# Retention steps of a fused retention and MoE kernel, placed by a written table instead of by run-ahead counters

## The chip, the core and the metric

The kernel runs on one core of a Trainium2 chip. A core has engines that each run their own instructions in order and wait for each other by semaphores: TensorE (PE in the profile; its weight loads are PEld), VectorE (DVE), ScalarE (ACT), GpSimd (POOL) and SyncE (SP). Transfers between device memory and on-chip memory (SBUF) are issued by SP, and here also by ACT, and run on 16 shared DMA engines. TensorE writes its results to the accumulation memory (PSUM), from which VectorE and ScalarE read them.

The metric is the device time of one execution in microseconds (us). The kernel before took 311.57 us, the median of 11 runs (310.76 to 315.99).

## The reference: what is computed

```python
scores = scale * np.matmul(q, k.transpose(0, 1, 3, 2))     # 8 batches, 8 heads, 576 positions, 64 wide
Dmat = np.where(rel >= 0, gamma[:, None, None] ** rel[None, :, :], 0.0)
attn = np.matmul(scores * Dmat[None], v)                   # retention: causal, decaying with distance
x = attn.transpose(0, 2, 1, 3).reshape(B * S, H * D)       # 4608 tokens, 512 wide
h = x @ w_in                                               # 512 -> 2048
g = h * np.clip(h + 3.0, 0.0, 6.0) / 6.0                   # hard swish
out = g @ w_out                                            # 2048 -> 512
```

Inputs and outputs are float32; inside, matrix operands are float16.

## The kernel before

**Retention by chunks.** Each of 8 batches has 576 positions: four chunks of 128 and a tail of 64. Two batches' tails make one tail chunk, so there are 36 chunks in `order` (0 to 35; 14, 23, 32 and 35 are tails). The decay is split into a factor on q and one on k and v, so that a chunk needs a causal mask and, from its second chunk of a batch on, a carried state. The steps of one chunk i have a letter each in what follows:

- **l**: three loads of q, k, v into tile `st` (SP, line 93; six of 64 rows for a tail, line 98). Six `st` buffers.
- **c**: three casts with the decay factors into `qk16` and `v16` (POOL, line 113). Five buffers of each.
- **x**: one DMA transpose of `qk16` into `qkT`, issued by ACT (line 121). Four buffers. The first eight chunks go through TensorE instead.
- **s** (`ret1`): 8 small matmuls to `sc` (line 150), then the mask on VectorE into `at` (line 157). `sc` has one buffer, so the next s waits for this mask.
- **o** (`ret2`): the matmuls of `at` with v and of the state with q into `xp` (lines 172, 178, 185), the state's update (line 197), then copies of `xp` into `xt` (line 202) and of the state (line 208) on ACT, or on VectorE for a batch's last chunk (line 210).

**The MoE by blocks.** 512 tokens make a block: block b holds the four full chunks of batch b, block 8 all tails. Blocks run in the order 0 to 6, 8, 7. Block 0 is done plainly, under the start-up loads. Each other block has an up part of 16 units and seven products:

- An up unit is 8 (`up_half`, 256 columns each, blocks 1 and 2) or 4 (`up`, 512 columns, the others) matmuls into one `mm` buffer of PSUM (lines 255, 241), then on ACT `u` (line 224) and on VectorE `g` (line 229). There are four `mm` buffers, shared with the products.
- The products P1, P5, P6, P2, P7, P4, P3 (line 353) are a Strassen form of the down matrix product: 16 matmuls each. Some need sums of g, made by `enc(kb, which, j0, j1)` on VectorE (line 317): written **e**kb.which.j0.j1 below. P5 reads sum 1, P6 sum 2 (which needs sum 1), P7 sum 3, P3 sum 4 (which needs sum 2). P5, P6, P7, P4 also read `tmat` 0 to 3, differences of the weights that `tbuild` makes once on VectorE (line 444): **t**2 and **t**3 fall into block 1. After P1 ACT copies X (line 359); after P6, P7, P4, P3 VectorE adds W, Z and the outputs (lines 362, 368, 376, 379, 382); after P2 ACT copies an output (line 373). Each of the last four products issues a store from SP (line 386).

**What sets the order.** The kernel is recorded under a manual schedule: each engine gets its instructions in the order in which the program writes them. Before, that order comes from counters: `burst()` writes s of chunk i+1, o of chunk i and then `ahead()`, which writes transposes up to three chunks ahead and casts up to four ahead, each cast followed by a load (`do_cast`, `do_load`). `burst` is called at fixed places: after up units 5 and 11, after some products (the sets given to `down`), and by `catch_up`. The sums of g stand at fixed places too. Each DMA of SP and ACT also takes one of eight completion counters in turn and waits until the earlier DMA on that counter has landed.

Of the kernel before, what the change touches and what calls it, by code (L numbers as in the profile page):

```python
# [18 lines left out]


E_H0, E_H = 316, 256
E_TAIL = 544


@with_exitstack
def kernel(
# [18 lines left out]
    NFC = DFF // P  # L45
# [96 lines left out]
    def ret1(c, nwarm=0):  # L142
        kind, b, t = c
        qt = qkTs[c]
        sc = psum.tile([P, 2, HP, P], FP32, tag="sc", name="sc")
        if nwarm:
            warm(sc[:, 0, 0, :], nwarm)
        for p in range(HP):
            for z in range(2):
                nc.tensor.matmul(sc[:, z, p, :],  # L150
                                 qt[z * D:z * D + D, HP + p, :],
                                 qt[z * D:z * D + D, p, :],
                                 start=True, stop=True)
# [3 lines left out]
        nc.vector.tensor_tensor(  # L157
            out=at.rearrange("p z a i -> p (z a) i"),
            in0=sc.rearrange("p z a i -> p (z a) i"),
            in1=m[:, :].unsqueeze(1).to_broadcast([P, 2 * HP, P]),  # L160
            op=ALU.mult)
# [134 lines left out]
    HF = NFC // 2  # L296
# [136 lines left out]
    def tbuild(which):  # L433
        if which == 0:
            a, c = wq(0, 1), wq(0, 0)
        elif which == 1:
            a, c = wq(1, 1), tmat[0]
        elif which == 2:
            a, c = wq(1, 1), wq(0, 1)
        else:  # L440
            a, c = wq(1, 0), tmat[1]
        for h in range(2):
            s = slice(4 * h, 4 * h + 4)
            nc.vector.tensor_tensor(out=tmat[which][:, s, :], in0=a[:, s, :],
                                    in1=c[:, s, :], op=ALU.subtract)


    order = []
# [6 lines left out]
    NCHK = len(order)  # L455
# [17 lines left out]
    for h in range(H):  # L473
        e = eq0 if h == 0 else eq
# [30 lines left out]
    def do_cast():  # L505
        if ncast[0] < NCHK:
            for ix in range(3):
                cast(order[ncast[0]], ix, GP)
            ncast[0] += 1
            do_load(ncast[0] + 6)  # L510

    def do_xp(tag=None, eng="v"):
        if nxp[0] < NCHK:
            if tag:
                xpose_pe(order[nxp[0]], tag, eng)
            else:
                xpose(order[nxp[0]])
            nxp[0] += 1

    def r1(i, nwarm=0):  # L520
        if i < NCHK:
            while nxp[0] <= i:
                do_xp()
            ret1(order[i], nwarm)

    def r2():
        if nb[0] < NCHK:
            ret2(order[nb[0]])
            nb[0] += 1

    def ahead():

        i = nb[0] - 1
        while nxp[0] < NCHK and nxp[0] <= i + 3 and nxp[0] < ncast[0]:
            do_xp()
        while ncast[0] < NCHK and ncast[0] <= i + 4:
            do_cast()

    def burst():
        if nb[0] < NCHK:  # L540
            r1(nb[0] + 1)
            r2()
            ahead()

    def catch_up(n):
        while nb[0] <= n:
            burst()


    c0 = order[:4]  # L550
# [66 lines left out]
            r2()  # L617
    down_plain_end(0, pos)
    do_xp("xp", "s")
    ahead()  # L620
    for w in range(8):
        up_half(1, 0, (w, w + HF))
        if w == 1:
            r1(7)
            r2()
            ahead()
        if w == 5:
            r2()
            ahead()
    for w in range(8):  # L630
        up_half(1, 1, (w, w + HF))
        if w == 1:
            ahead()
        if w in (4, 7):
            enc(1, 1, 0 if w == 4 else 4, 4 if w == 4 else 8)

    def down(kb, slots):
        enc(kb, 2, 0, 8)
        if kb >= 3:
            enc(kb, 3, 4, 8)  # L640
        for nm in ("P1", "P5", "P6", "P2", "P7", "P4", "P3"):
            product(kb, nm)
            if nm in slots:
                burst()
            if nm == "P1" and kb < 3:
                enc(kb, 3, 0, 8)
            if nm == ("P5" if kb > 1 else "P2"):
                enc(kb, 4, 0, 8)
            if kb == 1:
                if nm == "P1":  # L650
                    tbuild(2)
                if nm == "P5":
                    r1(8)
                if nm == "P6":
                    tbuild(3)

    def up_block(kb, slots):
        catch_up(need[kb])
        for fx in range(NFC):
            up(kb, (fx // 2) + (fx % 2) * HF)  # L660
            if fx in slots:
                burst()
            if fx == 9:
                enc(kb, 3, 0, 4)
                enc(kb, 1, 0, 4)
        enc(kb, 1, 4, 8)

    down(1, ("P7", "P4"))
    for w in range(8):
        up_half(2, 0, (w, w + HF))  # L670
        if w in (1, 5):
            burst()
    catch_up(need[2])
    for w in range(8):
        up_half(2, 1, (w, w + HF))
        if w in (4, 7):
            enc(2, 1, 0 if w == 4 else 4, 4 if w == 4 else 8)
    down(2, ("P1", "P6", "P2", "P7", "P4"))
    for kb in (3, 4, 5, 6, 8, 7):
        up_block(kb, (5, 11) if kb < 7 else ())  # L680
        down(kb, {3: ("P1", "P2"), 4: ("P1", "P2", "P4"), 5: ("P1", "P2"),
                  6: ("P1", "P6", "P2", "P7", "P4")}.get(kb, ()))


# [1 line left out]
_INS = ['q', 'k', 'v', 'moe_w_in', 'moe_w_out']  # L686
_OUTS = [((4608, 512), 'float32')]
# [25 lines left out]
```

## Time and profile before

| what | value |
|---|---|
| median of 11 runs | 311.57 us |
| the profiled execution: its own time | 313.4 us |
| its span, first to last instruction | 311.7 us |
| PE busy | 289.7 us (93%) |
| DVE busy | 234.3 us (75%) |
| ACT busy | 147.3 us (47%) |
| POOL busy | 119.6 us (38%) |
| mean granted TensorE clock | 0.989 |

The profile of one execution gives each engine's busy time, the waits (who waited for whom, by the semaphore that came last), the chain of work that ended last, a timeline of each engine, and tables by window. A matmul's busy time includes its pipeline, so single durations (273 ns for a 256-column matmul) are longer than the rate at which they follow each other (16 of them in 1.75 us). The stages of the profiled execution, read off PE's timeline: block 0 until 58.1 us, block 1 from 58.1 to 92.25, block 2 to 131.1, block 3 to 161.4, block 4 to 192.8, block 5 to 223.35, block 6 to 255.4, block 8 to 281.5, block 7 to 307.65, then the last output and its store.

### The profile page before, as it was taken

The page shows a single profiled execution, that of the slowest core. Times are in us where ns is not written, and L with a number is a line of the kernel's source. Part 1 is how long each engine was busy: PE and PEld are TensorE (multiplying, and loading weights), DVE is VectorE, ACT ScalarE, POOL GpSimd, SP SyncE. Part 2 cuts the span into 40 slices and gives each one's busy share as a digit, 9 for nine tenths or more (in the row PEclk, how much of TensorE's full clock was granted, in tenths as well). Part 3 has the DMA queues.
Part 4 walks back from the last instruction along what each step waited for, and adds up shares of the span by engine and source line. Part 5 has one row for each costly group of instructions (what it writes and reads, how often), then busy time and mean ns, then how long its engine had stood idle before and what let it go on. Part 6 is the DMA issues. An engine that isn't in the chain of part 4 may idle for free.

```text
span 311.7 us, 7065 instructions
## 1 busy us (share of the span) xinstructions
PE 289.7 (93%) x2848; PEld 199.5 (64%) x2848; DVE 234.3 (75%) x311; ACT 147.3 (47%) x277; POOL 119.6 (38%) x131
## 2 busy tenths in 40 slices
PE   1679999979999998799999999999999999999994
PEld 0465445768788886545874587458746874685583
DVE  4745749649978997489968986799689857956963
ACT  5474664746136733176327632763176326505610
POOL 5217518957175577533446327334610000000000
PEclk9988999999999999799999999999999999999999
DMA  9999999999999999999999999992511120014003
GB/s 167 218 350 387 377 207 216 203 186 225 255 203 199 230 216 207 249 188 188 206 212 206 220 243 175 242 210 47 170 34 36 36 105 33 1 27 102 8 2 135
DMA packets 155937, 53.94 MB, mean 173 GB/s; under 512 B 143104, under 2 KB 151296, under 8 KB 155904
## 3 DMA queue, kind: packets, MB, share of 16 engines
q1 hardware_dynamic: 126336, 46.15, 70.5%
q10 hardware_dynamic: 29568, 7.34, 18.2%
q8 instruction: 22, 0.36, 0.5%
q14 instruction: 11, 0.09, 0.1%
HBM read 36.70 MB, written 9.44 MB: 148 GB/s over the span
## 4 chain that ended last, share of the span: by engine, by line
PE 64%; DMA 12%; DVE 10%; issue 4%; SPq 4%; ACT 3%; POOL 1%; ACTq 0%; POOLq 0%
PE ph L241 24%; PE accC L353 9%; PE accB L353 7%; PE accA L353 7%; PE ph L255 5%; DMA st<-in_k_dram 5%; SPq L93 4%; PE accD L353 3%; DMA wst<-in_moe_w_out_dram 3%; DVE ss L317 3%; PE xp L172 3%; PE sc L150 3%; DMA qkT<-qk 2%; DVE at L157 2%; DMA st<-in_v_dram 2%
## 5 line engine op out<-in xcount | busy, mean ns | idle before, releaser
L229 DVE SCALAR_TENSOR_TENSOR g<-u,ph 128x512 f16<-128x512 f32 x144 | 95.6, 685 | 29.5 <-ACT u L224 28.7
L224 ACT ACTIVATE u<-ph 128x512 f32<-128x512 f32 x144 | 84.1, 597 | 67.8 <-PE ph L241 52.2
L241 PE MATMUL ph<-xt,win 128*128 128x512 f16 x384 | 85.6, 380 | 0.1
L241 PEld LDWEIGHTS <-win 128*128 128x128 f16 x448 | 43.3, 98 | 50.2 <-issue 0.6
L113 POOL TENSOR_TENSOR qk<-st,tq 128x512 f16<-128x512 f32 x30 | 32.9, 1096 | 61.2 <-issue 32.0
L113 POOL TENSOR_TENSOR v<-st,tkv 128x512 f16<-128x512 f32 x36 | 40.3, 1120 | 39.0 <-DMA st<-in_v_dram 22.3
L353 PEld LDWEIGHTS <-ss 128*128 128x128 f16 x512 | 49.5, 99 | 8.1 <-DVE ss L317 0.8
L157 DVE TENSOR_TENSOR at<-sc,mask 128x1024 f16<-128x1024 f32 x32 | 39.0, 1218 | 6.5 <-PE sc L150 6.2
L353 PEld LDWEIGHTS <-g 128*128 128x128 f16 x384 | 37.2, 98 | 5.7
L113 POOL TENSOR_TENSOR qk<-st,tkv 128x512 f16<-128x512 f32 x30 | 34.5, 1150 | 1.8 <-DMA st<-in_k_dram 1.8
L202 ACT ACTIVATE xt<-xp 128x512 f16<-128x512 f32 x32 | 19.2, 598 | 29.5 <-PE xp L178 25.3
L353 PE MATMUL accB<-tmat,ss 128*128 128x256 f16 x256 | 30.6, 273 | 0.7 <-DVE W L362 0.4
L255 PE MATMUL ph<-xt,win 128*128 128x256 f16 x256 | 29.1, 273 | 1.9 <-DVE g L229 1.9
L353 PE MATMUL accA<-wout,g 128*128 128x256 f16 x256 | 30.6, 273 | 0.0
L255 PEld LDWEIGHTS <-win 128*128 128x128 f16 x256 | 24.7, 98 | 5.0 <-issue 2.1
L317 DVE TENSOR_TENSOR ss<-g 128x1024 f16<-128x1024 f16 (+1 forms) x30 | 24.8, 843 | 0.3
L172 PE MATMUL xp<-at,v 128*64 128x128 f16 x288 | 20.7, 232 | 2.5 <-DVE at L157 2.5
L150 PE MATMUL sc<-qkT 64*128 64x128 f16 x288 | 14.9, 226 | 5.0 <-DMA qkT<-qk 2.1
L172 PEld LDWEIGHTS <-v 128*64 128x64 f16 x288 | 14.7, 114 | 6.8 <-issue 2.8
L373 ACT COPY osb<-accA 128x512 f32<-128x512 f32 x8 | 4.7, 586 | 29.6 <-PE accA L353 29.6
L150 PEld LDWEIGHTS <-qkT 64*128 64x128 f16 x288 | 8.6, 97 | 14.8 <-issue 9.7
L208 ACT CAST s<-state 64x256 f16<-64x256 f32 x48 | 17.3, 360 | 0.5
(61 smaller groups left out, 271.7 us busy)
## 6 DMA issues: line engine op xcount, KB each, us to landing
st<-in_q_dram SPq DMA_DIRECT2D x32, 256.0 KB, 5.3
st<-in_k_dram SPq DMA_DIRECT2D x32, 256.0 KB, 5.9
st<-in_v_dram SPq DMA_DIRECT2D x32, 256.0 KB, 6.4
out_dram<-osb SPq DMA_DIRECT2D x32, 256.0 KB, 4.1
wst<-in_moe_w_in_dram SPq DMA_DIRECT2D x4, 512.0 KB, 6.8
tmat<-in_moe_w_in_dram SPq DMA_DIRECT2D x4, 512.0 KB, 10.2
wst<-in_moe_w_out_dram SPq DMA_DIRECT2D x4, 512.0 KB, 9.8
g<-in_moe_w_out_dram SPq DMA_DIRECT2D x4, 512.0 KB, 10.8
```

The source lines that it names most:

```text
L113: eng.tensor_tensor(out=dst, in0=st[:, ix, :, :], in1=tab.unsqueeze(2).to_broadcast([P, H, D]), op=ALU.mult)
L150: nc.tensor.matmul(sc[:, z, p, :], qt[z * D:z * D + D, HP + p, :], qt[z * D:z * D + D, p, :], start=True, stop=True)
L157: nc.vector.tensor_tensor(out=at.rearrange("p z a i -> p (z a) i"), in0=sc.rearrange("p z a i -> p (z a) i"), in1=m[:, :].unsqueeze(1).to_ ...
L172: nc.tensor.matmul(xp[rows[z], p, :], vt[:, 2 * p + z, :], at[:, z, p, :], start=(p == 0), stop=False, skip_group_check=True)
L202: nc.scalar.activation(xts[b][:, :, t * P:(t + 1) * P], xp, ACTF.Copy, scale=0.125)
L208: nc.scalar.copy(s16[rows[z], :, rows[z]], sp[rows[z], :, :])
L224: nc.scalar.activation(u, ph, ACTF.Relu, bias=0.5, scale=1.0 / 6.0)
L229: nc.vector.scalar_tensor_tensor(out=dst, in0=uv, scalar=1.0, in1=pv, op0=ALU.min, op1=ALU.mult)
L241: nc.tensor.matmul(ph, win16[:, m, P * fc:P * fc + P], xt[:, m, :], start=(m == 0), stop=(m == NCC - 1))
L255: nc.tensor.matmul(ph[:, 256 * j:256 * j + 256], win16[:, m, P * fc:P * fc + P], xt[:, m, cs], start=(m == 0 and j == 0), stop=(m == NCC - 1),
L317: nc.vector.tensor_tensor(out=dst, in0=a, in1=c, op=op)
L353: nc.tensor.matmul(ps[:, m, :], lhs(fc, m), rhs[:, fc, :], start=(first and fc == 0 and m == 0), stop=(fc == HF - 1 and m == 1), skip_grou ...
```

## The change

The counters' helpers after block 0 (`ahead`, `burst`, `catch_up`, `up_block`, `down`) are gone. A table `STEPS` gives for each unit number a list of steps, written by letter as above, and one loop runs all units of blocks 1 to 8 in the same order as before and, after each unit, the steps listed for it. Unit 0 is ahead of block 1; a block has 23 units (16 up, 7 products), so block 1 is 1 to 23, block 2 is 24 to 46, block 3 is 47 to 69, and so on; block 8 is 139 to 161, block 7 is 162 to 184. The set of steps is the same as before, one for one: no instruction is added or removed on PE, DVE, ACT, POOL or SP. Only their places differ.

```diff
+STEPS = {
+    0: "c8 c9 l14 c10",
+    2: "o6 s7",
+    3: "x8",
+    4: "c11 l15",
+    6: "o7",
+    7: "x9 l16",
+    9: "x10 l17",
+    13: "t2",
+    15: "e1.1.0.4",
+    16: "e1.1.4.8 e1.2.0.8 s8",
+    17: "x11 t3 e1.3.0.8 c12",
+    19: "o8 s9 c13",
+    20: "x12 e1.4.0.8",
...
+    39: "e2.1.4.8 e2.2.0.8 o13 c18 s14 x16",
+    40: "x17 l24",
+    41: "e2.3.0.8",
+    42: "s15 o14 e2.4.0.8 c19",
+    43: "x18",
+    44: "o15 s16 l25",
+    45: "s17 o16 x19 c20",
...
+    125: "x34",
+    126: "o32 s33",
+    130: "c35 e6.3.0.4",
+    131: "e6.1.4.8 e6.2.0.8 s34 o33",
+    132: "e6.3.4.8 e6.4.0.8",
+    133: "x35",
+    135: "s35 o34",
+    137: "o35",
...
+}
...
-    def ahead():
-        i = nb[0] - 1
-        while nxp[0] < NCHK and nxp[0] <= i + 3 and nxp[0] < ncast[0]:
-            do_xp()
-        while ncast[0] < NCHK and ncast[0] <= i + 4:
-            do_cast()
-    def burst():
-        if nb[0] < NCHK:
-            r1(nb[0] + 1)
-            r2()
-            ahead()
...
+    def act(w):
+        n = [int(x) for x in w[1:].split(".")]
+        if w[0] == "s":
+            ret1(order[n[0]])
+        elif w[0] == "o":
+            ret2(order[n[0]])
+        elif w[0] == "x":
+            xpose(order[n[0]])
+        elif w[0] == "c":
+            for ix in range(3):
+                cast(order[n[0]], ix, GP)
+        elif w[0] == "l":
+            load(order[n[0]])
+        elif w[0] == "e":
+            enc(*n)
+        else:
+            tbuild(n[0])
+    def between():
+        for w in STEPS.get(unit[0], "").split():
+            act(w)
+        unit[0] += 1
...
+        for nm in ("P1", "P5", "P6", "P2", "P7", "P4", "P3"):
             product(kb, nm)
-            if nm in slots:
-                burst()
...
+            between()
```

The places in blocks 1 and 2, as both programs write them (u0 to u15 are up units; the number is the table's):

```
unit        before                                 after
 0          c8 l14 c9 l15                          c8 c9 l14 c10
 2  k1.u1   s7 o6 x8 x9 c10 l16                    o6 s7
 3  k1.u2                                          x8
 4  k1.u3                                          c11 l15
 6  k1.u5   o7 x10 c11 l17                         o7
 7  k1.u6                                          x9 l16
 9  k1.u8                                          x10 l17
13  k1.u12  e1.1.0.4                               t2
15  k1.u14                                         e1.1.0.4
16  k1.u15  e1.1.4.8 e1.2.0.8                      e1.1.4.8 e1.2.0.8 s8
17  k1.P1   e1.3.0.8 t2                            x11 t3 e1.3.0.8 c12
18  k1.P5   s8
19  k1.P6   t3                                     o8 s9 c13
20  k1.P2   e1.4.0.8                               x12 e1.4.0.8
21  k1.P7   s9 o8 x11 c12 l18                      l18
22  k1.P4   s10 o9 x12 c13 l19                     o9
25  k2.u1   s11 o10 x13 c14 l20                    s10 x13
26  k2.u2                                          l19
27  k2.u3                                          c14 l20
28  k2.u4                                          o10 s11
29  k2.u5   s12 o11 x14 c15 l21
30  k2.u6                                          o11 x14 s12 c15
31  k2.u7                                          l21
33  k2.u9                                          c16
34  k2.u10                                         o12 x15 s13 c17
36  k2.u12  e2.1.0.4                               e2.1.0.4 l22
37  k2.u13                                         l23
39  k2.u15  e2.1.4.8 e2.2.0.8                      e2.1.4.8 e2.2.0.8 o13 c18 s14 x16
40  k2.P1   s13 o12 x15 c16 l22 e2.3.0.8           x17 l24
41  k2.P5   e2.4.0.8                               e2.3.0.8
42  k2.P6   s14 o13 x16 c17 l23                    s15 o14 e2.4.0.8 c19
43  k2.P2   s15 o14 x17 c18 l24                    x18
44  k2.P7   s16 o15 x18 c19 l25                    o15 s16 l25
45  k2.P4   s17 o16 x19 c20 l26                    s17 o16 x19 c20
```

In blocks 3 to 6 the same steps stand a few units earlier or later, o often apart from s, and transposes alone between units; by the end of block 2 both programs have done s to 17 and o to 16. Block 6 ends with x34, x35, s34 and s35 as in the diff; before, x34 stood at unit 127 and s34 at 134, x35 at 132 and s35 at 135. In blocks 8 and 7 only four sums of g move by a few units.

More of the change, by code (lines that the diff above doesn't have):

```diff
@@ L21 @@
 E_H0, E_H = 316, 256
+STEPS = {
[12 more added lines that the diff above has]
+    20: "x12 e1.4.0.8",
+    21: "l18",
+    22: "o9",
+    25: "s10 x13",
+    26: "l19",
+    27: "c14 l20",
+    28: "o10 s11",
+    30: "o11 x14 s12 c15",
+    31: "l21",
+    33: "c16",
+    34: "o12 x15 s13 c17",
+    36: "e2.1.0.4 l22",
+    37: "l23",
+    39: "e2.1.4.8 e2.2.0.8 o13 c18 s14 x16",
[5 more added lines that the diff above has]
+    45: "s17 o16 x19 c20",
+    47: "c21",
+    49: "x20",
+    52: "o17 s18 l26",
+    54: "e3.3.0.4",
+    55: "x21 c22 e3.1.0.4",
+    56: "l27",
+    57: "l28",
+    58: "s19 o18",
+    62: "e3.1.4.8 e3.2.0.8",
+    63: "x22 c23 s20 o19",
+    64: "e3.3.4.8",
+    65: "x23",
+    66: "c24 e3.4.0.8",
+    68: "s21 o20",
+    69: "l29",
+    70: "c25",
+    71: "l30",
+    72: "l31",
+    73: "o21 s22",
+    74: "x24 c26 l32",
+    77: "e4.3.0.4 e4.1.0.4",
+    81: "o22 x25 s23",
+    83: "c27",
+    84: "l33",
+    85: "e4.1.4.8 e4.2.0.8 s24 x26 o23 c28 l34",
+    87: "e4.4.0.8",
+    88: "s25 o24 c29 x27",
+    89: "l35 e4.3.4.8",
+    90: "x28",
+    91: "o25 s26",
+    93: "c30",
+    95: "o26 s27",
+    100: "e5.1.0.4 x29",
+    102: "c31 e5.3.0.4",
+    104: "x30",
+    105: "s28 o27",
+    106: "c32",
+    108: "e5.1.4.8",
+    109: "e5.2.0.8 s29 o28",
+    110: "x31",
+    111: "e5.4.0.8 e5.3.4.8",
+    112: "s30 o29 c33 x32",
+    113: "c34",
+    114: "s31 o30",
+    118: "x33",
+    120: "o31 s32",
+    124: "e6.1.0.4",
+    125: "x34",
[6 more added lines that the diff above has]
+    137: "o35",
+    148: "e8.1.0.4",
+    154: "e8.1.4.8 e8.2.0.8 e8.3.4.8 e8.3.0.4",
+    156: "e8.4.0.8",
+    169: "e7.1.0.4",
+    172: "e7.3.0.4",
+    177: "e7.1.4.8 e7.2.0.8 e7.4.0.8",
+    179: "e7.3.4.8",
+}
 E_TAIL = 544
@@ L520, in r1 @@
     def r1(i, nwarm=0):
[L521 to L524 removed]
+        ret1(order[i], nwarm)
     def r2():
[L527 to L547 removed]
+        ret2(order[nb[0]])
+        nb[0] += 1
     c0 = order[:4]
@@ L619 @@
     do_xp("xp", "s")
[L620 to L640, printed above, removed]
+    unit = [0]
@@ L641, in down @@
+    between()
+    for kb in (1, 2, 3, 4, 5, 6, 8, 7):
+        if kb < 3:
+            for hb in range(2):
+                for w in range(8):
+                    up_half(kb, hb, (w, w + HF))
+                    between()
+        else:
+            for w in range(HF):
+                for z in range(2):
+                    up(kb, w + z * HF)
+                    between()
         for nm in ("P1", "P5", "P6", "P2", "P7", "P4", "P3"):
             product(kb, nm)
-            if nm in slots:
-                burst()
@@ L645, in down @@
[L645 to L682, printed above, removed]
+            between()
```

## The prediction

> **What bounds the kernel now.** I read the page first, for which engine is full and where it is not.
>
> ```profile
> PE   1679999979999998799999999999999999999994
> ...
> PEclk9988999999999999799999999999999999999999
> ```
>
> TensorE is at nine tenths from the fourth slice (7.8 us each) on, but for slices 9, 16 and 17, and the granted clock dips in slice 17. So I asked PE's own timeline for its gaps in blocks 1 and 2.
>
> ```profile
> 67.20 3.00 PE L255 MATMUL ph<-xt,win 128*128 128x256 f16 x26 [1.86 <-DVE g L229]
> ...
> 80.44 1.92 PE L353 MATMUL accB<-tmat,ss 128*128 128x256 f16 x16 [0.29 <-DVE ss L317]
> ...
> 118.72 0.40 PE L150 MATMUL sc<-qkT 64*128 64x128 f16 x8 [1.22 <-DVE at L157]
> ...
> 126.56 0.40 PE L150 MATMUL sc<-qkT 64*128 64x128 f16 x8 [2.12 <-DMA qkT<-qk]
> ...
> 127.59 3.53 PE L353 MATMUL accC<-wout,ss 128*128 128x256 f16 x16
> ```
>
> In brackets is the idle time and who ended it. The last line is block 2's P3: 16 matmuls that take 1.75 us elsewhere took 3.46 in the chain. The table of windows says why, the granted clock (the number 0.50) was half:
>
> ```profile
> 128.00:130.00 2.00, 2.00 (x11) 1.44 (x10) 0.97 (x3) 0.16 (x1) 2.00 (x3) 0.50 1.34 251
> ```
>
> From 131.1 on there is no gap worth a name: the chain runs through PE to 307.65. Next, what the gaps waited for. ACT's timeline ahead of the first:
>
> ```profile
> 61.25 1.34 ACTq L121 DMA_TRANSPOSE qkT<-qk  x1
> ...
> 62.70 3.03 ACTq L121 DMA_TRANSPOSE qkT<-qk  x1
> 65.83 2.06 ACT L224 ACTIVATE u<-ph 128x512 f32<-128x512 f32 x4 [3.62 <-POOL qk L113]
> ```
>
> x8 and x9, issued back to back, held ACT for 4.4 us; u waited, then g, then PE. VectorE's timeline in the products of blocks 1 and 2:
>
> ```profile
> 78.44 1.95 DVE L317 TENSOR_TENSOR ss<-ss,g 128x2048 f16<-128x2048 f16 x1
> 80.31 1.21 DVE L317 TENSOR_TENSOR ss<-g 128x2048 f16<-128x2048 f16 x1
> 81.44 1.28 DVE L444 TENSOR_TENSOR tmat<-wout 128x1024 f16<-128x1024 f16 x2
> 82.65 1.21 DVE L157 TENSOR_TENSOR at<-sc,mask 128x1024 f16<-128x1024 f32 x1
> ...
> 113.02 1.93 DVE L317 TENSOR_TENSOR ss<-g 128x2048 f16<-128x2048 f16 x1
> 114.87 2.06 DVE L317 TENSOR_TENSOR ss<-g,ss 128x2048 f16<-128x2048 f16 x1
> 116.86 0.68 DVE L362 TENSOR_TENSOR W<-accB,X 128x512 f32<-128x512 f32 x1
> 117.46 1.21 DVE L157 TENSOR_TENSOR at<-sc,maskt 128x1024 f16<-128x1024 f32 x1
> ```
>
> It runs without a break, and the mask that s15 waits for (117.46) stands behind two sums. The sums are 1.21 us alone and 1.9 to 2.1 with POOL casting beside them (its casts at 113.83 and 115.81 took 2.02 each against 1.04).
>
> **The change, part by part.** Nothing is added or removed, so the sum is over gaps. TensorE has no cover: its work sets the end, and a gap there counts in full.
>
> *Block 1, up.* x8 and x9 are four units apart now. A transpose alone holds ACT's queue 1.25 us (median of 28), while a unit takes PE 0.875 and u 0.60: the next u is about 0.45 us late, and PE, up to four `mm` buffers ahead, has some 1.2 us (three units, 2.6, less u and g with their hand-over, 1.4). So nothing is lost. What is late next is VectorE. PE's up part would be 16 x 0.875 + o6, s7 (1.03) + o7 (0.70), from 58.1 to 73.9; the g of its thirteenth unit, at 71.3, is done 1.5 later, at 72.8. Then VectorE's own list: t2 1.28, two g 1.38, a half sum 0.69, g 0.69, half sum 0.69, sum 2 1.22 (1.95 beside casts): 78.75 to 79.5. P6 needs sum 2. It began at 80.44 before. From there PE needs P6, o8 and s9 (0.80), P2, P7, P4, o9 (0.70), P3: five products at 1.75, 1.50, about 0.4 for four switches (a product behind a chunk's step reads 1.85 in the chain, not 1.75), and 0 to 0.7 because W, behind mask, t3 and sum 3, frees P7's buffer late: block 1 ends at 89.5 to 90.9, after 31.4 to 32.8 us. I take 32.4, near the contended end: POOL was busy with c12 at that time in the trace of before (75.4 to 79.3). x10 comes 2 us behind x9; if it is slow as x9 was, up to 1.0 more.
>
> *Block 2.* Before, 92.25 to 131.12 is 38.87 us, and its gaps are 1.22 (s15), 2.12 (s17) and 1.71 (P3 at half clock), 5.05 together. s17 waited for x17, written behind o14 and two products ahead of s17, 4.5 us, where the transpose lands 6.2 us after its issue. Now x17 follows P1, with four products and s15, o14, o15, s16 between: some 10.8 us. s15 stands behind P6, and its mask behind W, no longer behind sums 3 and 4 both. PE's sum: up 14.0, products 12.25, s10 to s17 8 x 0.33 = 2.64, o10 to o16 5 x 0.70 + 0.47 + 0.60 = 4.57, eight switches 0.8: 34.3. VectorE's: 16 g 11.0, eight masks 9.8, four state copies 1.7, W, Z and outputs 3.45, sums 5.0: 31.0, one tenth less, so single waits remain: o11 on a mask written two units ahead (0.2), P6 on sum 2 (0 clean, 0.7 contended). I take 34.8, between 34.5 and 35.2. s10 (0.43) is in it, and was in block 1 before.
>
> *Blocks 3 to 8.* They took 176.5 us. Counting the same steps at the same rates (blocks 3 and 5 at 29.95, 4 at 30.9, 6 at 31.5, 8 and 7 at 26.1) gives 174.5, and some 20 switches at 0.1 are 2.0 more: nothing is left to gain but single tenths. New tight places: x31 to s31, four products and s30, o29 (8 us) for a landing of 5 to 6; x34 to s34, six units' 5.2 less 0.7 that ACT is behind, plus o32 and s33 (0.9), about 5.4; x35 to s35, 4.6 because ACT reaches x35 right behind X of P1. The four transposes after 215 us landed in 3.1 to 4.8, so none of these waits. Taken at 0; bounds: 1.5 better (each block loses its leftover), 2.0 worse (s34 and s35 wait at the median of all, 6.1: 0.7 and 1.5).
>
> *Casts and loads.* POOL's order of casts is unchanged, and each starts when its load has landed and o has freed its buffers, so their place in the table moves nothing. On SP the loads keep their order; stores pass loads at a few places: load 19 now goes behind all four stores of block 1 instead of three, load 29 behind all four of block 3's instead of none. Load 19 is worked out to land at 114 to 117 and cast 19 needs o14 at 114, x19 at 122: covered by 5 us. Load 29 has 20 us or more. Should SP fall behind, a transpose waits on ACT for the load eight DMAs ahead of it; the nearest is x13 on load 14's k: landed about 90, x13 at 91.2 or later. If that cover goes, 1 us.
>
> **Sum.** Blocks 1 and 2: 73.0 before, 32.4 + 34.8 = 67.2 after. Saved 5.8. The profiled execution's own 313.4 becomes 307.6; the median of the runs is 1.8 below that execution, so 311.57 - 5.8 = **305.8 us**.
>
> The clock term is the doubtful one. In this trace a gap of 1.86 us left the clock whole and one of 2.12 was followed by half clock, and 1.71 of the 5.8 is this. The Trainium skill (TensorE: Matmul & The Clock Gate, Part 1 on the HAM clock gate, and the table in Why this matters for your kernels) speaks against that reading: it lets the clock fall only after an idle window of about 3.4 us and advises against gaps over about 3 us, so neither gap should have mattered, and without this term the sum would be 4.1 us and the time 307.5. I go by the row.
>
> **The rivals.**
>
> *Slow transposes (ends slower).* If a transpose between up units takes 3.03 us as x9 did, u comes 2.2 late, PE's lead of 1.2 is gone, and 1.0 us is lost at each. The table has 14 transposes between up units. From six such losses on it eats the gain; at 14 it ends at 305.8 + 14 = 320, at 9 around 315. For it: 198.91 (2.02) and 149.86 (2.44) were slow too, and SP's issues beside them. Against: three of 28 over 2 us, none of them costing PE more than 0.2 but for the pair.
>
> *VectorE stays the bound (less gain).* Should every sum of blocks 1 and 2 meet a cast (0.8 for each of six) and half of that reach PE, 2.4 of the gain goes, 308.2; with x10's 1.0, 309.2. For it: VectorE's 31.0 against 34.3. Against: the casts run 3 us per chunk, less than half the time.
>
> *It does not do what it says.* 13 transposes stood between up units before and 14 do now, in ScalarE's busiest stretches. If then only the pair x8, x9 is cured and s15, s17 find other waits as long: 1.9 saved, 309.7. Against: x17's lead of 10.8 us is in the order itself.
>
> *More gain.* No contention and blocks 3 to 8 lose their leftovers: 31.4 + 34.5 saves 7.1, with 1.5 more 8.6: 303.0.
>
> **How the numbers follow.** Chances: forecast (304.5 to 307.7) 0.52, more gain 0.14, VectorE bound 0.18, not as it says 0.06, slow transposes 0.10. The range leaves out the slow transposes and about half of the smallest gains: 302.8 to 310.0, the bounds above nearly. The forecast's own range is 304.5 to 307.7. A difference under 0.5% (1.56 us) is about what a measurement can't tell from none: faster is under 310.0. From the cases: 0.52 + 0.14 + 0.16 + 0.02 = 0.84 faster, 0.06 same, 0.10 slower.
>
> **What would show it.** Right: PE's timeline of blocks 1 and 2 without the waits on transposes and at (118.72, 126.56), clock 1.00 from block 1 on, P6 of block 1 starting near 79, block 3 at 125 to 126, later blocks as long as before. Wrong: ACTq transposes of 2 to 3 us with PE idle on g behind them; s34 or s35 waiting on a landing; a second half-clock stretch.

## The result, and the profile after

The changed kernel took 309.64 us (median of 13 runs, 308.64 to 310.28) beside 312.18 for the kernel before on the same chips (48 runs). The ratio is 0.991, with a 95% interval of 0.9884 to 0.9936: 0.9% faster. That is the forecast direction and inside the range of 302.8 to 310.0, but 2.5 us where 5.8 (1.9%) were forecast. The profiled execution took 310.28 us; its span is 308.6 (311.7 before).

PE's and the clock's rows of the page after:

```profile
PE   1679989999899999989999999999999999999994
...
PEclk9999999999999999999999999999999999999998
```

PE's slices 9 and 17, which stood at 7 in the kernel before, are at 9, and so is the clock's slice 17. Two later slices have fallen from 9 to 8: the eleventh, with a wait of P6 in block 1, and the eighteenth, in block 3. Where the stages end, read from the end of each block's last product in PE's timeline (us, and length of the block):

| block | before | after |
|---|---|---|
| 1 | 92.25 (34.2) | 90.82 (32.7) |
| 2 | 131.12 (38.9) | 125.36 (34.5) |
| 3 | 161.44 (30.3) | 158.54 (**33.2**) |
| 4 | 192.80 (31.4) | 189.89 (31.4) |
| 5 and 6 | 255.41 (62.6) | 252.28 (62.4) |
| 8 and 7 | 307.64 (52.2) | 304.52 (52.2) |

Blocks 1 and 2 end 5.8 us earlier, as forecast. Block 3 gives 2.9 of it back. PE's timeline of block 1's P6 and of block 3, only the rows with an idle time in brackets:

```profile
80.20 1.92 PE L454 MATMUL accB<-tmat,ss 128*128 128x256 f16 x16 [0.93 <-DVE ss L418]
...
133.66 2.75 PE L342 MATMUL ph<-xt,win 128*128 128x512 f16 x12 [1.20 <-DVE g L330]
136.58 1.89 PE L342 MATMUL ph<-xt,win 128*128 128x512 f16 x8 [0.17 <-DVE g L330]
140.97 2.75 PE L342 MATMUL ph<-xt,win 128*128 128x512 f16 x12 [0.51 <-DVE g L330]
143.89 1.91 PE L454 MATMUL accA<-wout,g 128*128 128x256 f16 x16 [0.17 <-DVE g L330]
```

The brackets of block 3 add up to 2.05 us. A matmul's busy time includes its pipeline, so the starts tell more: matmuls that follow each other start 0.22 us apart here, and at these four places the distance is 2.7 us longer in all. PE waits for g, which waits for u. ScalarE's timeline of the same stretch says why u is late:

```profile
126.08 1.25 ACTq L222 DMA_TRANSPOSE qkT<-qk  x1
127.44 1.58 ACT L325 ACTIVATE u<-ph 128x512 f32<-128x512 f32 x3 [3.41 <-POOL qk L214]
130.94 1.25 ACTq L222 DMA_TRANSPOSE qkT<-qk  x1
132.28 1.58 ACT L325 ACTIVATE u<-ph 128x512 f32<-128x512 f32 x3 [3.27 <-POOL qk L214]
...
138.18 1.32 ACTq L222 DMA_TRANSPOSE qkT<-qk  x1
139.60 1.58 ACT L325 ACTIVATE u<-ph 128x512 f32<-128x512 f32 x3 [3.02 <-PE state L298]
```

These are x19, x20 and x21. Each time three u, whose matmuls are long done, stand behind a transpose that hasn't issued. What the transposes wait for is not what the brackets name (POOL had cast chunk 19's k by 122.08, chunk 20's by 127.12, chunk 21's by 131.98). GpSimd's timeline has rows that start at the same moments, released by loads:

```profile
126.08 1.04 POOL L214 TENSOR_TENSOR qk<-st,tkv 128x512 f16<-128x512 f32 x1 [1.01 <-DMA st<-in_k_dram]
...
130.94 1.04 POOL L214 TENSOR_TENSOR qk<-st,tkv 128x512 f16<-128x512 f32 x1 [1.30 <-DMA st<-in_k_dram]
...
138.25 1.09 POOL L214 TENSOR_TENSOR v<-st,tkv 128x512 f16<-128x512 f32 x1 [0.36 <-DMA st<-in_v_dram]
```

These casts belong to later chunks: k of chunk 20, k of chunk 21 and v of chunk 22. In the built program a DMA's completion is counted on one of eight counters in turn, and a DMA waits until the one before it on its counter, the eighth DMA ahead, has landed. The count goes by the order of the built program, in which x19 stands between k and v of load 22; it can't be read off the table's places. The waits written there are x19 on chunk 20's k, x20 on chunk 21's k and x21 on chunk 22's v. By the semaphore records of the trace these three landed at 126.01, 130.87 and 138.12, and the transposes were issued 0.06 to 0.07 us later. In the kernel before, x17 to x21 were issued 3.8 us or more after the last such landing. SyncE's timeline shows that these loads were late; the three rows after, and the same three loads before:

```profile
119.33 1.91 SPq L194 DMA_DIRECT2D st<-in_k_dram  x1
...
124.51 1.10 SPq L194 DMA_DIRECT2D st<-in_k_dram  x1
...
131.80 1.34 SPq L194 DMA_DIRECT2D st<-in_v_dram  x1
```

```profile
114.19 0.94 SPq L93 DMA_DIRECT2D st<-in_k_dram  x1
...
118.64 2.42 SPq L93 DMA_DIRECT2D st<-in_k_dram  x1
...
126.56 2.13 SPq L93 DMA_DIRECT2D st<-in_v_dram  x1
```

An issue took 1.1 to 2.9 us here, and these three landed 6.3 to 6.7 us after their issue began. Before, load 20 (its q first) began at 113.72 and load 22 at 122.41 on SyncE; after, at 116.40 and 126.90, while block 3 began 5.8 us earlier.

So theory A: the transposes of block 3 hold ScalarE until the eighth DMA ahead has landed, because the loads keep their own pace and PE has moved ahead of it. Rival B: x20 and x21 only stand too early for their own casts (in the trace above those were done 3.8 and 6.2 us before the issue, which already speaks against it). Rival C: the order of sums, masks and steps in blocks 3 to 8 costs the 2.9 us itself.

### The profile page after: what moved, and what is told of

Read it like the earlier page. It is cut to its first block, busy times and chain, and to the rows that moved or that the text cites. A ratio compares the mean times of both kernels' runs of the same rounds, so it can differ in the third digit from the quotient of the medians.

```text
span 308.6 us, 7061 instructions
## 1 busy us (share of the span) xinstructions
PE 288.2 (93%) x2848; PEld 197.0 (64%) x2848; DVE 233.5 (76%) x311; ACT 146.1 (47%) x277; POOL 119.8 (39%) x131
## 4 chain that ended last, share of the span: by engine, by line
PE 65%; DMA 15%; SPq 8%; DVE 6%; issue 1%; POOL 1%; ACT 1%; ACTq 0%; POOLq 0%
PE ph L342 23%; PE accB L454 8%; SPq L194 8%; PE accC L454 8%; PE accA L454 8%; PE ph L356 4%; DMA st<-in_v_dram 4%; PE accD L454 4%; PE po L383 3%; DMA st<-in_k_dram 3%; DMA wst<-in_moe_w_out_dram 3%; DVE g L330 3%; PE xp L273 3%; PE sc L251 2%; DMA st<-in_q_dram 2%; DMA wst<-in_moe_w_in_dram 2%
## 5 line engine op out<-in xcount | busy, mean ns | idle before, releaser
L214 POOL TENSOR_TENSOR qk<-st,tq 128x512 f16<-128x512 f32 x30 | 34.2, 1140 | 53.6 <-PE state L298 17.9
L454 PEld LDWEIGHTS <-ss 128*128 128x128 f16 x512 | 48.8, 98 | 9.1 <-DVE ss L418 3.2
L214 POOL TENSOR_TENSOR v<-st,tkv 128x512 f16<-128x512 f32 x36 | 40.2, 1116 | 33.2 <-DMA st<-in_v_dram 24.0
L214 POOL TENSOR_TENSOR qk<-st,tkv 128x512 f16<-128x512 f32 x30 | 33.2, 1105 | 5.8 <-DMA st<-in_k_dram 5.7
L418 DVE TENSOR_TENSOR ss<-g 128x1024 f16<-128x1024 f16 (+1 forms) x30 | 25.8, 865 | 0.3
L454 PE MATMUL accC<-tmat,ss 128*128 128x256 f16 x128 | 15.5, 273 | 0.6 <-DVE ss L418 0.6
```

The costliest lines, as they stand in the source:

```text
L214: eng.tensor_tensor(out=dst, in0=st[:, ix, :, :], in1=tab.unsqueeze(2).to_broadcast([P, H, D]), op=ALU.mult)
L418: nc.vector.tensor_tensor(out=dst, in0=a, in1=c, op=op)
L454: nc.tensor.matmul(ps[:, m, :], lhs(fc, m), rhs[:, fc, :], start=(first and fc == 0 and m == 0), stop=(fc == HF - 1 and m == 1), skip_grou ...
```

## The experiments

Times are medians; "block 3" is one profiled execution's length of it.

**One at a time: places, order, bytes, the transposes.** The first group ran beside a kernel before of 311.46 us.

```diff
e1_late_x   -    49: "x20",            +    52: "o17 s18 l26 x20",
            -    55: "x21 c22 ...",    +    58: "s19 o18 x21",
e3_rest     units 0 to 46 of STEPS: the steps where the kernel before has them
e4_halfv    + nh = 4 if ix == 2 and 15 <= order.index(c) <= 22 else H
            + src[b, 0:nh, ...]        # and two half casts of v from these four heads
e5_no_x     -    49: "x20"  +    49: "y20"   -    55: "x21 ..."  +    55: "y21 ..."
            + elif w[0] == "y": qkTs[order[n[0]]] = qkTs[order[19]]
```

> The changed kernel with x20 and x21 put back to the units at which they stood before (52 and 58 instead of 49 and 55). Theory A (a DMA holds ScalarE's queue until the eighth DMA ahead of it has landed, and the loads on SP are late in block 3): three units later, eight DMAs back is a later load too (part of load 22 and of load 23), so the hold stays in some form; 309 to 311 us, within 1 us of the changed kernel, block 3 still 32 us or more. Rival B (x20 and x21 only stand too early for their own casts): their hold goes, block 3 comes back to 30.3, the time 2 to 3 us under the changed kernel.

Measured: 309.35 us, ratio 0.991 (0.9879 to 0.9941), as the changed kernel in time. But the profiled execution, its fastest (307.39), has block 3 at 30.9, where A had said 32 or more. B is no better: x20 issued at 131.88, when chunk 20's k had been cast since 124.0; it was held 1.3 us past the end of the u before it (130.61), and chunk 22's q, the eighth DMA ahead, landed at 131.82. So the hold is there, but block 3 is only 0.6 us over 30.3. Chunk 20's k had also been issued at 115.48 in this execution instead of 119.33. A was right on the hold and wrong on block 3 in this execution; what the median one lost, 2.0 us longer, no profile shows.

> The table of before up to unit 46, that of the changed kernel from unit 47 on. Theory A (the hold in block 3 comes from where loads and stores stood in blocks 1 and 2): block 3 stays at about 30.3 us and the time is that of before within 1 us, 311 to 313. Rival C (the order of sums, casts and steps in blocks 3 to 8 itself costs the 2.9): blocks 1 and 2 as before, block 3 near 33, 314 to 315.

Measured: 312.01 us, ratio 1.0035 (0.9998 to 1.0073), block 3 at 30.3. The places from unit 47 on cost nothing when blocks 1 and 2 run as before: C as a cause by itself is out. (The profiled execution was a long one, 315.99, by two half-clock stretches in blocks 1 and 2, which are told of below.)

> The changed kernel in which v of the chunks 15 to 22 is loaded for heads 0 to 3 only and used for heads 4 to 7 again: it leaves half of v's bytes of eight chunks out (8 x 128 KB, a sixth of these loads), and no instruction of an engine. Theory A, with the DMAs' rate as the cause of the lag: the loads catch up by about 0.9 us a chunk, block 3 falls from 33.2 to 30.3 to 31 and the time by 2 to 3 us. Theory A with SP's issue time as the cause (as many issues as before): less than 1 us. Rival C (order of the sums): no change.

Measured: 308.79 us, ratio 0.9914 (0.9882 to 0.9946), block 3 at 31.7: 1.5 us of the 2.9. Load 22 was issued at 121.52 instead of 126.90, yet x19 and x20 were issued at 125.59 and 129.93, only 0.5 and 1.0 us earlier, and x21 at 134.64, 3.5 earlier. In this program other DMAs stand eighth ahead (chunk 21's v for x19, chunk 22's v for x20): earlier data frees a transpose less when the count moves along. The time is 0.9 us under the changed kernel's by the medians and not at all by the ratios, so neither branch of the expectation came out clearly; that fewer bytes brought load 22 forward by 5.4 us speaks for bytes, and not only the number of issues, setting the loads' pace.

> The changed kernel without the transposes of chunks 20 and 21 (their scores and states read chunk 19's transposed tile; the rest is computed). Theory A: two of the holds of ScalarE are gone, block 3 falls to 30.5 to 31.5, the time 1.5 to 2.5 us under the changed kernel. Rival C: as the changed kernel within 0.5 us.

Measured: 307.50 us, ratio 0.988 (0.9829 to 0.993), block 3 at 30.3 with no wait of PE over 0.3. Without the two transposes the whole loss is gone. It is not all theirs, though: in this execution chunk 20's k landed at 124.13 instead of 126.01, and x19 was issued at 124.21, ahead of block 3, so its hold cost nothing either. The run s1_look below tells the shares apart. The median is 2.1 under the changed kernel's, the ratio only 0.3% under its ratio, and the two intervals overlap. C is out by this too, since every sum and step of block 3 stands where the changed kernel has it.

**The changed kernel again, and three moves.** The second group ran beside 313.35 us before.

```diff
after_again no change
g1          -    45: "s17 o16 x19 c20",  +    45: "s17 o16 x19 c20 x20",
            -    62: "e3.1.4.8 e3.2.0.8", +   62: "e3.1.4.8 e3.2.0.8 x21",   # x20, x21 gone from 49, 55
g3_stores   osb: bufs=4 -> bufs=6; block 1's stores kept in a list and written by
            -    26: "l19",   +    26: "l19 h2",      -    40: "x17 l24",  +    40: "x17 l24 h2",
e6_pair     -     3: "x8",  -     7: "x9 l16",  +     2: "o6 s7 x8 x9",  +     7: "l16",
```

> The changed kernel once more, unchanged, to stand beside the others on one chip. The three runs of the first group have shown that block 3 falls back to 30.3 us without x20 and x21 and stays there with the old table ahead of it. Theory A: the same holds on ScalarE again, x18 to x21 issuing within 0.3 us of the landing of the eighth DMA ahead, block 3 at 31.5 to 33.5 us, the time 0.8 to 1.0% under before. If block 3 is at 30.5 here, the loss is an accident of one execution and the time in the first result has another cause.

Measured: 309.61 us (309.07 to 309.83), ratio 0.9885 (0.9843 to 0.9926), block 3 at 33.2 again. x19 and POOL's k cast began at 125.79 and 125.78, x21 and POOL's v cast at 137.74 and 137.81. x20 was issued at 130.58, where no row of POOL begins, but chunk 21's k had landed at 130.52. The hold isn't an accident.

> The changed kernel with x20 right behind x19 (unit 45, in the products of block 2) and x21 behind block 3's up part (unit 62): no transpose stands ahead of a u in block 3. Theory A: the holds stay, but they fall where ScalarE has little to do; block 3 at 30.3 to 31.5, the time 1 to 2 us under the changed kernel; x20 waits for its eighth DMA ahead (part of load 20), and the first u of block 3 may be late by up to 1.5 us, which is the doubt. Rival B (x20 merely too early for its cast): x20, now earlier still, holds ScalarE until its cast at about 128.5, block 3's first u come 2 us late, no faster than the changed kernel.

Measured: 311.84 us, ratio 0.9966 (0.9932 to 1.0), 2.2 us slower than the changed kernel where A had expected a gain, with block 3 at 35.2. ScalarE's timeline, and PE's:

```profile
125.87 4.36 ACTq L221 DMA_TRANSPOSE qkT<-qk  x2
130.33 2.06 ACT L324 ACTIVATE u<-ph 128x512 f32<-128x512 f32 x4 [6.80 <-issue]
```

```profile
131.70 1.87 PE L341 MATMUL ph<-xt,win 128*128 128x512 f16 x4 [3.38 <-DVE g L329]
```

The table of windows (the number before the last two is the granted clock):

```profile
130.00:132.00 2.00, 0.30 (x1) 0.10 (x1) 1.04 (x2) 1.67 (x4) 1.75 (x2) 0.74 1.03 228
132.00:134.00 2.00, 2.00 (x6) 0.73 (x5) 1.44 (x3) 0.79 (x2) 1.04 (x1) 0.50 1.29 253
134.00:136.00 2.00, 2.00 (x29) 1.01 (x28) 1.12 (x2) 1.26 (x4) 0.49 (x1) 0.90 1.39 210
```

Two transposes back to back held ScalarE 4.36 us, as x8 and x9 did before (1.34 and 3.03), PE idled 3.38 us and then ran at half clock. Both things that the change cured in blocks 1 and 2 came back at another place. The 4.36 is issuing, not waiting: the two issues took 2.54 and 1.71 us, and what x20 needs, chunk 20's k cast and chunk 20's v landed, was there at 126.9 and 127.1, before x19's issue was over at 128.4. So B's reason, x20 waiting for its own cast, isn't what cost here. Of the 12 executions 10 had a clock of 0.994 or less.

> The changed kernel with six output buffers, and block 1's four stores put behind load 19 (two) and load 24 (two). Loads 18 to 23 are issued 2 to 4 us earlier by it; the transposes stay where they are. Theory A: the DMAs eight ahead of x18 to x21 land earlier by as much, ScalarE's holds shrink, block 3 comes to 30.5 to 31.5 and the time 1.5 to 2.5 us under the changed kernel. Rival C (order of the sums in block 3) or B (casts late): no change, within 0.5 us.

Measured: 308.23 us (308.01 to 308.54), ratio 0.9843 (0.9802 to 0.9884), 1.4 us under the changed kernel of the same group, all six runs below its fastest. Block 3 is 31.1; x18 to x21 issued at 117.97, 124.71, 129.80 and 136.15, 1.1 to 2.1 us earlier than in the first profile of the changed kernel (0.8 to 1.6 than in the one of this group), with load 22 at 124.28. The stores out of the way moved the loads, and the loads moved the transposes: A, with a gain 0.1 under its bound. The count moved here too (x19 waited for chunk 20's v and x20 for chunk 21's v, and each was issued 0.07 us after that landing). This version beats both kernels.

> The changed kernel with x8 and x9 side by side again behind the second unit of block 1, as before. The prediction's step for block 1: PE waits 1.86 us on g at the seventh unit again, of which the later steps of the block keep 1 to 1.9; block 1 ends near 92.5 instead of 90.8. What reaches the end is less if block 3 waits for DMAs that keep their own time (theory A: 0 to 1 us of it), all of it if not.

Measured: 309.73 us, ratio 0.9894 (0.9848 to 0.9941), 0.1 over the changed kernel. PE waited 1.37 us on g at 66.6, and block 1 ended at 91.60, 1.2 later than in the other profile of this group (90.43); then block 3 took 32.3 instead of 33.2. At the start of block 3 PE was 1.4 us late, at its end 0.4: most of what was lost in block 1 came back, since the holds end when the loads land, whenever PE gets there. That is strong support of A: the cure of the pair x8, x9 is worth 0.1 us by the medians as things stand.

**Off ScalarE, and one part alone.** The third group ran beside 312.15 us before, the fourth (s1_look, s5, g9) beside 311.66.

```diff
s1_sp       x20, x21: nc.scalar.dma_start_transpose -> nc.sync.dma_start_transpose ("z")
            -    37: "l23", - 49: "x20", and l24, l25, x21 from 40, 44, 55
            -    47: "c21",   +    47: "c21 z20 l23 z21 l24 l25",
s4_both     g3_stores and s1_sp together: 47: "c21 z20 l23 z21 l24 h2 l25"
b_x17       the kernel before, "s14 o13 x16 c17 l23", "s15 o14 x17 c18 l24"
            ->                 "s14 o13 x16 c17 x17 l23", "s15 o14 c18 l24"
g4          g3_stores, t2 from unit 13 to 17 (behind x11), t3 from 17 to 19
s5          s4_both, t2 and t3 as g4, x30 from unit 104 to 108
g9          g4, x20 to 52, x21 to 58, x30 to 108
```

> The changed kernel with the transposes of chunks 20 and 21 issued by SyncE behind loads 22 and 23 instead of by ScalarE between the up units of block 3 (loads 23 to 25 written behind the casts of chunk 21 for it). The DMAs are the same and wait for the same landings, but ScalarE is not held by them. Theory A: no u of block 3 stands behind a transpose; block 3 falls from 33.2 to 30.3 to 31 us and the time by 2 to 2.9 us, to 306.7 to 307.7. What could spoil it: x20 issued at about 133 to 135 lands at 140, five before s20. Rivals B (own casts late) and C (order of the sums): no change, within 0.5 us.

Measured: 309.00 us, ratio 0.989 (0.985 to 0.993): 0.6 under the changed kernel by the medians and nothing by the ratios, where 2 to 2.9 was expected. The profiled execution took 340.45 us at a mean clock of 0.858; block 3 is read from the next run of the same kernel.

> The changed kernel with the transposes of chunks 20 and 21 on SyncE again, for a profile of an undisturbed execution: its median was 309.0 us, 0.6 under the changed kernel, where 2 to 2.9 were expected. Theory A1 (holds move on): block 3 at 30.3 to 31, and 1 to 2.3 us lost in a later block behind a transpose that ScalarE issues there, as x30 in block 5 of the kernel with both edits. Theory A2 (x20 on SyncE comes too late): block 3 still 32 to 33 us, with s20 or s21 waiting for the landing of a transpose.

Measured: 309.11 us (two runs), block 3 at 31.6. ScalarE's timeline and PE's:

```profile
126.50 2.04 ACTq L220 DMA_TRANSPOSE qkT<-qk  x1
128.64 1.57 ACT L323 ACTIVATE u<-ph 128x512 f32<-128x512 f32 x3 [4.52 <-PE ph L340]
```

```profile
130.01 1.89 PE L340 MATMUL ph<-xt,win 128*128 128x512 f16 x8 [1.09 <-DVE g L328]
```

Neither A1 nor A2: x20 and x21 cost nothing on SyncE (issued at 135.85 and 141.73), and later blocks are as they were, but x19, still on ScalarE ahead of block 3, is held to 126.50, 0.08 us after chunk 20's k landed, and PE loses 1.1 us to it. So x20 and x21 carried 1.6 of the 2.9; most of the rest is x19's. That the time fell by less than block 3 did isn't explained.

> The kernel with block 1's stores put off (second group), with the transposes of chunks 20 and 21 on SyncE as well, the second two stores behind load 24. Theory A: block 3 at 30.3 to 30.8, so 0.3 to 0.8 us under the kernel with the stores put off alone, 307.4 to 307.9, and about as the one with the two transposes on SyncE: both take away the same loss and don't add up.

Measured: 308.27 us (306.93 to 308.82), ratio 0.9861 (0.9822 to 0.99). Block 3 is 30.3 as A said, and the two edits don't add up, as it said too; but the time is that of g3_stores, not 0.3 to 0.8 us under it. In the profiled execution, the slowest, block 5 took 33.5 instead of 31.2, behind x30:

```profile
200.57 1.25 ACTq L220 DMA_TRANSPOSE qkT<-qk  x1
201.92 0.60 ACT L323 ACTIVATE u<-ph 128x512 f32<-128x512 f32 x1 [3.85 <-POOL qk L212]
```

ScalarE had nothing else since 198.1, and chunk 34's q, the eighth DMA ahead of x30, landed at 200.49. PE, now ahead in block 5 as well, meets the loads' pace there. In the changed kernel x27 and x30 were held in the same way (issued 0.07 and 0.08 us after their landings, at 182.36 and 201.33), but PE's timeline shows no wait behind block 3.

> The kernel before, with one transpose moved: x17 stands one product earlier, behind x16 and ahead of the copies of o14. ScalarE issues it at about 121 instead of 122.8. The prediction's step for block 2: the wait of s17 (2.1 us) falls to 0 to 0.6, and the half clock behind it goes; a profile shows block 2 at 35.5 to 37 us instead of 38.9. The median falls by 1.5 to 3 us. If the clock is what scatters the times of before, the executions over 314 us go, apart from those with a half clock behind the 1.9 us wait of block 1. If the clock was full all the same in most executions, the median falls by 1.5 or less. If theory A hands it back in block 3, block 3 is longer than 30.3.

Measured: 311.38 us (310.08 to 313.29), ratio 0.9974 (0.9944 to 1.0003), unclear. (The 122.8 of the expectation is x18's issue; x17 was issued at 119.84 before, and at 118.47 here.) In the profile block 2 is 36.0 us (38.9 before), without s17's wait and at full clock, as the step said, and block 3 is 30.3. No execution was over 314. But the median fell by 0.8 only, which is the branch "the clock was full all the same in most executions".

> The kernel with block 1's stores put off (second group), with t2 and t3 moved behind the first sums of block 1, so that VectorE reaches sum 2, which P6 waits for, about 1.2 us earlier: block 1 ends 0.6 to 1.2 us earlier. Theory A: the loads keep their own time, so that block 3 is longer by as much and the end within 0.4 us of the kernel with the stores put off alone (308.2). If blocks 1 and 2 still set the end: 0.6 to 1.2 us less, 307.0 to 307.6.

Measured: 308.10 us (307.04 to 310.66), ratio 0.9874 (0.9824 to 0.9924), as g3_stores (308.23). It doesn't test A: block 1 ended at 90.95 in its profile, not earlier (91.14), because its P3 then waited 1.2 us at 89.0 for VectorE's output sum over `accC`: VectorE's list hadn't got shorter, and t3, 2.4 us with casts beside it, now stood in front of that sum instead of in front of sum 2.

> The kernel with both edits (block 1's stores put off, x20 and x21 on SyncE), with t2 and t3 behind the first sums of block 1 and x30 moved from the twelfth to the last up unit of block 5, where no u stands behind it. Theory A1: block 3 at 30.3 to 30.8, block 5 at 31.2 instead of 33.5, the time 306 to 307.5 us. If something else sets block 5 (its sums, the loads of chunk 34 late for their cast), it stays at 33 and the time at 308.

> The kernel with block 1's stores put off and t2, t3 later, with x20 and x21 at units 52 and 58 as before the change and x30 behind the last up unit of block 5; all transposes on ScalarE. Theory A: ScalarE is free of the holds of two units each that it would meet at 49 and 55, block 3 at 30.3 to 30.9 instead of 31.1, the time 307.3 to 308.0 us, a few tenths under the kernel with the stores put off.

Measured: s5 308.94 us (307.47 to 310.0), ratio 0.9892 (0.9841 to 0.9943); g9 308.40 (307.31 to 308.73), ratio 0.9863 (0.9819 to 0.9908). In both profiles block 3 is 30.3 and block 5 31.2, so no hold costs PE anything there any more, though some are left (in g9 x20 was issued at 132.95, 0.09 us after the landing that it waits for). The spans are 305.8 and 306.7. Yet the medians are not below g3_stores, and above what was expected. The profiled execution of s5 is its fastest, and the others take up to 2.5 us longer at a clock of 1.0, in a place that no profile shows. That stays open.

Of all versions g3_stores is the one to keep: none is clearly below it, and it leaves the transposes on ScalarE. The Trainium skill (DMA: Bandwidth & Descriptors, Silent corruption: two transposing streams in flight at once) says that transposes issued from two engines' queues must not be in flight together. No run here shows that effect: with x20 and x21 on SyncE the built program has waits between the two queues, and in s1_look x20 was issued at 135.85 after x19 had landed (132.15), and x22, on ScalarE, at 146.28 after x21 had (146.18).

## Why the prediction was wrong in size

**Blocks 1 and 2: right.** Forecast 67.2 us, measured 67.3 (32.7 and 34.5). Two slips in the working did no harm: between x17 and s17 stand five products, not four (the 10.8 us is the sum with five), and x17 landed 6.7 us after its issue in the kernel before, not 6.2. P6 began at 80.20 (forecast about 79, contended 79.5); no gap on a transpose is left in the two blocks, s15 and s17 wait for nothing over 0.2, and the 0.93 us that P6 still waits is the VectorE list that the step had counted.

**"Casts and loads": the step that failed.** It named the very mechanism ("a transpose waits on ACT for the load eight DMAs ahead of it") and then priced it at x13 alone, with 1 us if the cover went, and covered load 19 "by 5 us". The cover went because the loads were worked out too early: load 19 was to land at 114 to 117 and landed at 119.96 to 122.79. In the trace SyncE's issues took 1.1 to 2.9 us, load 20 began 2.7 us and load 22 4.5 us later than before, and block 3 began 5.8 us earlier. x13 was not held (load 14's k landed at 88.2, x13 was issued at 92.66); x18 to x21 were, and block 3 took 33.2 us instead of 30.3: 2.9 us that the sum had at nothing. The sum was made of PE's gaps as if the loads would follow PE's new pace; they kept their own.

**"Blocks 3 to 8 ... taken at 0": right but for that.** With the steps of blocks 3 to 8 in their new places and the old blocks ahead of them, nothing changes (e3_rest: block 3 30.3, ratio 1.0035). The five blocks behind block 3 (4, 5, 6, 8, 7) took 146.0 us after and 146.2 before; s34 and s35 didn't wait. The upper bound of 2.0 was meant for those two and was exceeded by another cause.

**The clock term and the median: right in the execution, wrong in the sum.** After the change no gap of PE from block 1 on is over 1.25 us, and no half clock follows, as forecast. But the 5.8 us, with 1.71 of half clock in it, was taken off the median of the runs, 1.8 us below the profiled execution, and the distance was kept. That distance is about one such stretch, which the median execution doesn't have. The runs of the kernel before beside the experiments speak for it (61 executions):

| granted clock | executions | median |
|---|---|---|
| 0.997 to 1.0 | 34 | 311.44 us |
| 0.991 to 0.996 | 21 | 313.53 us |
| 0.99 and below | 6 | 315.46 us |

A median of 311.57 goes with an execution without such a stretch: there was nothing of the 1.71 to save in it. By this table that is likely, not shown, since the table doesn't tell where a stretch lies. The profiled execution's 0.989 holds two: besides the one behind s17 there is one in block 0, from 21.7 to 25.1 us, which the prediction passed over, though its own clock row has an 8 in the third and the fourth slice (granted clock again before the last two numbers):

```profile
21.00:22.00 1.00, 0.15 (x4) 0.18 (x6) 0.71 (x1) 0.95 (x3) 0.00 (x0) 0.85 1.06 399
22.00:23.00 1.00, 1.00 (x24) 1.00 (x22) 0.00 (x0) 0.59 (x2) 0.00 (x0) 0.50 1.04 391
...
25.00:26.00 1.00, 1.00 (x5) 0.39 (x4) 0.00 (x0) 0.01 (x1) 0.68 (x2) 0.95 1.05 385
```

The profiled executions of e4_halfv and s1_look hold a stretch at the same place and were the fastest of their runs, so there it seems to cost little. Of the changed kernel's 19 executions 17 were at 0.997 or more, so what the clock term gives is the end of the long executions: 308.64 to 310.28 instead of 310.56 to 316.74. The Trainium skill (TensorE: Matmul & The Clock Gate, Part 1 on the HAM clock gate) calls the window over which the clock is decided free-running, about 3.4 us long, with a count of slow matmuls at a kernel's start that differs from run to run; the table, with 0 to 2 stretches in one and the same program, agrees with that much.

Together: 305.8, plus 1.7 that the median execution never had, plus 2.9 in block 3, less 0.2 in the blocks behind it, is 310.2. The profiled execution, from which the last two are read, took 310.28; the median is 309.64, and these 0.6 us stay open. e6_pair adds that the first cure, priced at 1.9 us of PE time, moves the end by 0.1 while block 3 waits for loads.

**The rivals.** Slow transposes did not come as worked out (after a single transpose between units u was late by less than PE's lead); what came is close kin, a transpose that holds ScalarE before its issue instead of during it. VectorE was not the bound in block 3: every wait of PE there is on a g, and the largest ones follow a held u.

## What to carry to other kernels

When a change takes gaps out of the bounding engine, ask whether the transfers keep up with its new pace: a stretch in which the loads are already late hands the gain back at the next place where something waits for a landing. In a program that counts its DMAs on a few counters in turn, a DMA that is issued from a compute engine's queue may be held by another DMA's landing, with all of that engine's work behind it; put it where the engine has time, and look in the built program for what stands ahead of it on its counter. And before a term is taken off a median, look whether the profiled execution is like the median one, here by its clock.

## What was not expected of the hardware

- Half-clock stretches have one length. The sum of the missing clock over one-microsecond windows is 1.71 us behind the gap of 2.12 (kernel before), 1.70 behind that of 3.38 (g1), and 1.70 behind each of those of 1.99 and 2.24 (e3_rest): 3.4 us at half speed each time. Gaps of 1.86 (kernel before), 1.54 (b_x17) and 1.37 us (e6_pair) left the clock whole. That does not make 1.9 us a limit. By the clock's records in the trace, stretches of one execution start a whole number of 3.413 us steps apart (21.69 and 127.51 in the kernel before, 31 steps). On that grid the gap of 1.86, from 65.34 to 67.20, is cut in two at 66.06, while the gaps of 2.12, 1.99 and 2.24 each lie whole in the step ahead of their stretch. The gap of 1.54 lies whole in one step too; so what these runs leave open for idle time within a step is 1.54 to 1.99 us.
- Two DMA transposes issued one behind the other from one queue held it 4.5 us (x8 and x9 before) and 4.4 us (x19 and x20 in g1), where a single one mostly takes 1.25. It isn't the place: in the changed kernel x23, issued 0.2 us behind x22's issue, took 4.06, and x28 behind x27 2.92, both where PE had no wait for it.
